# Loading one of four weight blocks through ScalarE's DMA queue in place of SyncE's, at the start of a gated attention and gMLP kernel

## The chip, the cores and the metric

The kernel runs on one core of one Trainium2 chip. The metric is the device time of one execution in microseconds. A profiled execution also has a span, from its first to its last instruction; where both are known, the time is the span plus about 1.7 us (206.23 against 204.5 in the profiled execution of before).

Every trace here shows a mean granted TensorE clock of 0.998 or more. All timed runs count as fast.

## The reference, cut to what matters

```python
g = sigmoid((x * gate_w).sum(-1, keepdims=True))
a = A(x)                       # linear attention with softmax features, 32 heads
z = gelu(x @ w_in)             # [2048, 512] @ [512, 1376]
z1, z2 = z[..., :688], layernorm(z[..., 688:])
b = (z1 * (w_sp @ z2 + b_sp)) @ w_out
out = g * a + (1 - g) * b
```

The experiment concerns only the first step: the columns 688 to 1375 of `w_in`, which give `z2`. They are loaded in four blocks of 128 rows, and a tile is 128 rows of x.

## The kernel before

Five kinds of data are needed at the start: tiles 0 and 1 of x (loaded as they are and transposed on TensorE), four blocks of w_in, the gate row, tiles 2 and 3 of x (transposed by the DMA itself), and the other half of w_in. Two engines issue these transfers, SyncE (`nc.sync`) and ScalarE (`nc.scalar`).

```python
def load_z2w(eng, dt):                                     # L117
    eng.dma_start(out=w_z2[:, dt, 0:FH], in_=w_in_v[:, dt, FH:F])

nc.sync.dma_start(out=xs[:, 0, :], in_=x2[0:P, :])         # L119
nc.scalar.dma_start(out=xs[:, 1, :], in_=x2[P:2 * P, :])   # L120
load_z2w(nc.sync, 0)
load_z2w(nc.scalar, 1)
load_z2w(nc.sync, 2)
nc.scalar.dma_start(out=gaterow[0:NDT, :], in_=gate_w...)  # L124
load_z2w(nc.sync, 3)
nc.scalar.activation(out=scrap[:, :], ..., func=AF.Gelu_apprx_tanh)   # L127, loads the table
x_dma_T(2, 2)                                              # L131, x tiles 2 and 3
for h in range(2):
    nc.sync.dma_start(out=w_z1[:, 2*h:2*h+2, :], ...)      # L135, the other half of w_in
...
```

TensorE first runs seven dummy matmuls (L222), then transposes x tiles 0 and 1 (L280). It then works through the blocks in their order, for both tiles, and goes on to tile 2 (matmuls of L191 and L230):

```python
warm_up(6); warm_up(1, P)
x_T(0, ...); x_T(1, ...)
one(0, 0, 0); z_part(0, 0, HF, True); gate_T()     # one(tile, block, half)
one(0, 1, 0); one(1, 0, 0); z_part(1, 0, HF, True); one(1, 1, 0)
... one(tt, 1, 1) ...                              # block 1
... one(tt, 2, 0); one(tt, 2, 1); z_part ...       # block 2
... one(tt, 3, 0); one(tt, 3, 1); z2_out ...       # block 3
z2_tile(2); z2_tile(3)                             # needs the DMA transpose of L131
```

The softmax here doesn't subtract the row's maximum and nothing guards it: scores larger than these inputs give would overflow.

Of the kernel before, what the change touches and what calls it, by code (L numbers as in the profile page):

```python
# [35 lines left out]
def kernel(  # L36
# [14 lines left out]
    nc = tc.nc  # L51
# [64 lines left out]
    def load_z2w(eng, dt):  # L116
        eng.dma_start(out=w_z2[:, dt, 0:FH], in_=w_in_v[:, dt, FH:F])  # L117
# [4 lines left out]
    load_z2w(nc.scalar, 1)  # L122
    load_z2w(nc.sync, 2)
    nc.scalar.dma_start(out=gaterow[0:NDT, :], in_=gate_w.rearrange("(dt p) -> dt p", p=P))  # L124
    load_z2w(nc.sync, 3)
    scrap = early.tile([P, 1], BF16, name="scrap")
    nc.scalar.activation(  # L127
        out=scrap[:, :], in_=nc.const_aps.tensor(1.0, [P, 1], BF16), func=AF.Gelu_apprx_tanh)
# [515 lines left out]
```

## Time and profile before

| | before |
|---|---|
| median of the three runs known before the prediction | 206.92 us (206.57 to 206.94) |
| span of the profiled execution | 204.5 us |
| TensorE busy | 200.6 us, 98% |
| transpose of x tiles 2 and 3 issued / landed | 2.67 / 7.23 us |
| tile 2 starts on TensorE | 7.27 us |

Times inside an execution count from its first instruction. A landing is the moment at which a transfer's semaphore is complete. Landings are given to 0.01 us from the records of the trace; the DMA view rounds the time from issue to landing to 0.1 us. The profiled execution of before took 206.23 us.

### The profile page before, as it was taken

What the parts mean: (1) busy time and instruction counts of PE and PEld (TensorE: products, weight loads), DVE (VectorE), ACT (ScalarE), POOL (GpSimd) and SP (SyncE); (2) the same over time, 40 slices, a digit from 0 to 9 for tenths busy, and PEclk for the clock granted to TensorE, in tenths of its full rate; (3) what the DMA queues carried; (4) which work ended last, traced back from release to release, by engine and by line L of the source; (5) the groups of instructions that cost most, each with busy time, mean ns of one, the idle gap of its engine ahead of it and who ended that gap; (6) DMA issues with size and microseconds to landing.
All of it is one profiled execution on the core that took longest, in us unless ns stands there. A gap on an engine that the chain in (4) does not pass through costs nothing.

```text
span 204.5 us, 3996 instructions
## 1 busy us (share of the span) xinstructions
PE 200.6 (98%) x1557; PEld 119.5 (58%) x1557; DVE 130.5 (64%) x283; ACT 74.6 (36%) x122; POOL 45.8 (22%) x76
## 2 busy tenths in 40 slices
PE   8999999999999999999999999999999999999994
PEld 3566666655665555656565666555555555665642
DVE  4567484837977587979797788555566645633332
ACT  3466678796222333332424042222251136002303
POOL 3020202021523325334242442222204220200000
PEclk9999999999999999999999999999999999999999
DMA  5998599999997017950422229763567458552943
GB/s 188 247 209 151 117 277 209 241 194 234 207 290 168 3 38 148 317 97 15 77 47 46 51 38 114 142 126 62 108 161 79 90 112 184 61 96 51 141 80 104
DMA packets 89931, 27.22 MB, mean 133 GB/s; under 512 B 84184, under 2 KB 89912, under 8 KB 89912
## 3 DMA queue, kind: packets, MB, share of 16 engines
q1 hardware_dynamic: 87744, 24.99, 64.1%
q10 hardware_dynamic: 2168, 1.98, 3.6%
q8 instruction: 12, 0.20, 0.4%
q14 instruction: 7, 0.06, 0.1%
HBM read 4.15 MB, written 2.10 MB: 31 GB/s over the span
## 4 chain that ended last, share of the span: by engine, by line
PE 95%; DMA 2%; SPq 1%; DVE 0%; issue 0%
PE mm L454 37%; PE zp L191 17%; PE mm L355 14%; PE mm L515 8%; PE mm L509 7%; PE mm L395 7%; DMA xT<-in_A_x_dram 2%; PE kvacc L411 2%; PE at L467 2%; PE mm L520 1%; SPq L117 1%; PE zp L307 0%; PE at L478 0%; SPq L119 0%; PE pq L307 0%; DVE ob L527 0%
## 5 line engine op out<-in xcount | busy, mean ns | idle before, releaser
L454 PE MATMUL mm<-z2all,wspT 128*128 128x344 bf16 x512 | 79.9, 309 | 0.0
L454 PEld LDWEIGHTS <-wspT 128*128 128x128 bf16 x512 | 49.0, 98 | 25.3
L191 PE MATMUL zp<-w_z,xT 128*128 128x344 bf16 (+1 forms) x254 | 38.2, 309 | 0.3 <-DMA xT<-in_A_x_dram 0.3
L359 ACT ACTIVATE eq<-mm 128x512 bf16<-128x512 f32 x32 | 17.4, 594 | 51.4 <-PE mm L355 25.7
L363 DVE TENSOR_REDUCE zs<-eq 128x64 f32<-128x1024 bf16 x16 | 19.5, 1220 | 20.1 <-ACT eq L359 20.1
L191 PEld LDWEIGHTS <-xT 128*128 128x128 bf16 x254 | 24.3, 98 | 12.4 <-DMA xT<-in_A_x_dram 0.6
L359 ACT ACTIVATE ek<-mm 128x512 bf16<-128x512 f32 x32 | 17.3, 600 | 27.1 <-PE mm L355 27.1
L459 DVE SCALAR_TENSOR_TENSOR ucat<-mm,bT,z1all 128x344 bf16<-128x344 f32 x32 | 17.4, 544 | 15.1 <-PE mm L454 15.1
L372 POOL TENSOR_TENSOR eq<-eq,ratio 128x512 bf16<-128x512 bf16 x16 | 16.9, 1059 | 44.6 <-DVE ratio L371 36.6
L531 ACT ACTIVATE ob<-mm,g_inv 128x512 bf16<-128x512 f32 (+1 forms) x15 | 10.1, 680 | 33.1 <-PE mm L520 28.5
L363 DVE TENSOR_REDUCE zs<-ek 128x64 f32<-128x1024 bf16 x16 | 19.3, 1209 | 2.8 <-ACT ek L359 2.8
L515 PE MATMUL mm<-wspT,uT 128*128 128x512 bf16 (+2 forms) x85 | 20.1, 367 | 0.0
L355 PEld LDWEIGHTS <-xT 128*128 128x128 bf16 x128 | 12.2, 98 | 12.0
L372 POOL TENSOR_TENSOR ek<-ek,ratio 128x512 bf16<-128x512 bf16 x16 | 16.9, 1059 | 2.2 <-DVE ratio L371 1.7
L509 PE MATMUL mm<-wspT,oT 128*128 128x512 bf16 (+2 forms) x68 | 16.6, 366 | 0.0
L355 PE MATMUL mm<-wq_p,xT 128*128 128x512 bf16 x64 | 16.4, 379 | 0.0
L395 PE MATMUL mm<-wv_sb,xT 128*128 128x512 bf16 x64 | 16.4, 379 | 0.0
L355 PE MATMUL mm<-wk_p,xT 128*128 128x512 bf16 x64 | 16.3, 379 | 0.0
L209 DVE BATCH_NORM_STATS2 bn<-z2all 128x6 f32<-128x344 bf16 x32 | 14.9, 501 | 0.0
L206 ACT ACTIVATE z2all<-zp 128x688 bf16<-128x688 f32 x16 | 11.8, 744 | 7.6 <-PE zp L191 7.6
L260 ACT ACTIVATE z1all<-zp 128x688 bf16<-128x688 f32 x16 | 11.9, 744 | 5.1 <-PE zp L191 4.6
L515 PEld LDWEIGHTS <-uT 128*128 128x128 bf16 x85 | 8.1, 98 | 9.4 <-issue 0.2
(77 smaller groups left out, 141.8 us busy)
## 6 DMA issues: line engine op xcount, KB each, us to landing
out_dram<-ob ACTq DMA_DIRECT2D x12, 128.0 KB, 2.7
wspT<-in_B_w_out_dram SPq DMA_DIRECT2D x2, 640.0 KB, 5.5
w_z<-in_B_w_in_dram SPq DMA_DIRECT2D x2, 344.0 KB, 4.8
w_z<-in_B_w_in_dram SPq DMA_DIRECT2D x3, 172.0 KB, 3.6
wv_sb<-in_A_wqkv_dram SPq DMA_DIRECT2D x2, 256.0 KB, 4.0
wspT<-in_A_wo_dram SPq DMA_DIRECT2D x2, 256.0 KB, 4.1
out_dram<-ob SPq DMA_DIRECT2D x3, 128.0 KB, 1.8
uT<-ucat SPq DMA_TRANSPOSE x16, 2.8
```

Source lines behind the costliest of these rows:

```text
L191: nc.tensor.matmul(zp[:, j, 0:n], lhsT=xT[:, dt, tt * P:(tt + 1) * P], rhs=wt[:, dt, j * HF:j * HF + n], start=(dt == 0), stop=(dt == NDT ...
L209: nc.vector.bn_stats(out=bn6[:, tt, j, :], in_=z2v[:, j, :])
L260: nc.scalar.activation(out=z1all[:, tt, :].rearrange("p (j n) -> p j n", j=2), in_=zp[:, :, 0:HF], func=AF.Gelu_apprx_tanh,)
L355: nc.tensor.matmul(ps[:, :], lhsT=xT[:, dt, tt * P:(tt + 1) * P], rhs=w[:, dt, :], start=(dt == 0), stop=(dt == NDT - 1))
L359: nc.scalar.activation(out=e[:, :, a, :], in_=ps[:, :].rearrange("p (h f) -> p h f", f=DH), func=AF.Exp, scale=1.0 - 2.0 * a)
L363: nc.vector.tensor_reduce(out=z[:].rearrange("p h a -> p (h a)"), in_=e[:].rearrange("p h a f -> p (h a) f"), axis=AX.X, op=ALU.add,)
L372: nc.gpsimd.tensor_tensor(out=e[:, :, 1, :], in0=e[:, :, 1, :], in1=ratio[:, :, None].to_broadcast([P, H, DH]), op=ALU.mult)
L395: nc.tensor.matmul(v_ps[:, :], lhsT=xT[:, dt, tt * P:(tt + 1) * P], rhs=wv_sb[:, dt, :], start=(dt == 0), stop=(dt == NDT - 1))
L454: nc.tensor.matmul(gp[:, 0:HF], lhsT=wspT[:, st, tt * P:(tt + 1) * P], rhs=z2all[:, st, j * HF:(j + 1) * HF], start=(st == 0), stop=(st == ...
L459: nc.vector.scalar_tensor_tensor(out=ucat[tt % NU][:, c0 + j * HF:c0 + (j + 1) * HF], in0=gp[:, 0:HF], scalar=bT[:, tt:tt + 1], in1=z1all[ ...
L509: nc.tensor.matmul(acc, lhsT=oTs[tt][:, g, :], rhs=wo_t[:, g, c0:c1], start=start and g == 0, stop=stop and g == NG - 1)
L515: nc.tensor.matmul(acc, lhsT=uTs[tt][:, i + ft, :], rhs=w_main[i][:, ft, c0:c1], start=start and ft == 0, stop=False)
```

## The change

The change wants to take one issue of 0.43 us off SyncE, so that the transpose for x tiles 2 and 3 and everything behind it is issued earlier.

```diff
     nc.scalar.dma_start(out=gaterow[0:NDT, :], in_=gate_w.rearrange("(dt p) -> dt p", p=P))
-    load_z2w(nc.sync, 3)
+    load_z2w(nc.scalar, 3)
```

## The prediction

> **What bounds the kernel now.** I read the page first: its engine shares, its slices and its chain of work.
>
> ```profile
> span 204.5 us, 3996 instructions
> PE 200.6 (98%) x1557; PEld 119.5 (58%) x1557; DVE 130.5 (64%) x283; ACT 74.6 (36%) x122; POOL 45.8 (22%) x76
> ...
> PE 95%; DMA 2%; SPq 1%; DVE 0%; issue 0%
> ```
>
> TensorE is busy for 200.6 us of 204.5, and the chain that ended last lies on it for 95%. Only 2% of the chain is a DMA and 1% SyncE's issuing, and both are in the first microseconds. So the second view is the chain of waits in the window from 0 to 8 us (start, duration, what).
>
> ```profile
> 0.81 0.40 SPq L119
> 1.21 0.06 issue
> 1.26 0.42 SPq L117
> 1.68 0.05 issue
> 1.73 0.42 SPq L117
> 2.15 0.04 issue
> 2.20 0.43 SPq L117
> 2.63 0.04 issue
> 2.67 4.55 DMA xT<-in_A_x_dram
> 7.23 0.05 issue
> 7.27 0.76 PE zp L191 x4
> ```
>
> SyncE issues one load of x and then blocks 0, 2 and 3 of w_in, at 1.26, 1.73 and 2.20 us. Only then, at 2.67, does it issue the transpose that loads x tiles 2 and 3. That transpose lands at 7.23, and TensorE starts tile 2 at 7.27. The issue of block 3, 0.43 us and a gap of 0.04, is thus a link of the chain, and it is what the change takes out.
>
> How much is there to gain? The third view is the timeline of TensorE around that point.
>
> ```profile
> 5.17 0.89 PE L191 MATMUL zp<-w_z,xT 128*128 128x344 bf16 x5
> ...
> 6.25 0.74 PE L191 MATMUL zp<-w_z,xT 128*128 128x344 bf16 x4
> 7.27 0.91 PE L191 MATMUL zp<-w_z,xT 128*128 128x344 bf16 x5 [0.28 <-DMA xT<-in_A_x_dram]
> ```
>
> The page shows 309 ns for one such matmul, but they overlap: four take 0.74 us, so one starts every (0.74 - 0.31) / 3 = 0.144 us. The last of the four started at 6.25 + 3 x 0.144 = 6.68 and its successor could have started at 6.83. It started at 7.27. The stall is therefore 7.27 - 6.83 = 0.44 us, not just the 0.28 us of visible idle. The table of waits of TensorE has only one other entry, 0.8 us before the first instruction. The windows view has TensorE busy for 16.53 us of the 16.53 us from 7.27 to 23.80, and for 60.00 of the 60.00 us from 40 to 100. What is won at 7.27 has no later wait to vanish in. Its most is 0.44 us, 0.2% of the time.
>
> [...] The trace has this time: 0.42 us for a load of 172 KB. So I count no bandwidth as won. [...] The DMA view from 2 to 4 us agrees with the sharing:
>
> ```profile
> q1 hardware_dynamic: 284, 0.31, 50.7%
> q10 hardware_dynamic: 281, 0.30, 41.8%
> ```
>
> q1 is SyncE's queue and q10 ScalarE's: with work in both they moved 0.31 and 0.30 MB. [...] the trace has 1.28 us for it at 2.35 us. I need that number because the change pushes this load back.
>
> **The change part by part.** The order view (before against after) shows 3116 rows on TensorE, all alike, and no difference on VectorE and GpSimd. On SyncE three loads in a row become two; on ScalarE one load appears between the gate row and the table load. Bytes, tiles and matmuls are the same. The waits that the later SyncE issues carry are the same too.
>
> Removed from SyncE: one issue, 0.43 + 0.04 = 0.47 us. The transpose is then issued at 2.67 - 0.47 = 2.20. Its issue lasts 1.45 us, to 3.65. The next issue, half of the other weights, waits for both loads of x; these land 2.7 and 2.9 us after 0.81 and 0.80, so at 3.5 and 3.7. It moves from 4.17 to about 3.70. If the landing moves with the issue, tile 2 is there at 7.23 - 0.47 = 6.76, just ahead of the 6.83 at which TensorE could use it, and the whole 0.44 us is won.
>
> Added to ScalarE:
>
> ```profile
> 1.24 0.47 ACTq L117 DMA_DIRECT2D w_z<-in_B_w_in_dram  x1
> 1.75 0.57 ACTq L124 DMA_DIRECT2D gaterow<-in_gate_w_dram  x1
> 2.35 1.28 ACT L127 ACT_TABLE_LOAD   x1 [2.35 <-DVE ident L112]
> 3.65 0.21 ACT L127 ACTIVATE scrap<-const-bfloat16-1.0 128x1 bf16<-128x1 bf16 x1
> 4.46 0.37 ACT L283 COPY xT<-pq 128x256 bf16<-128x256 bf16 x1 [0.61 <-PE pq L280]
> ```
>
> The issue of block 3 stands at about 2.35 and takes 0.47 us by the row of block 1. The table load goes to 2.35 + 0.50 = 2.85, ends at 4.13, and the scrap activation ends at about 4.36. ScalarE's first useful work, the copy of x, starts at 4.46 after an idle 0.61 us. The 0.50 us fits into that idle time with 0.1 us to spare. ScalarE costs nothing.
>
> Moved: block 3 is issued at 2.35 in place of 2.20, 0.15 us later, on the other queue. This is the delicate part. It landed 4.0 us after its issue, at 6.2, and TensorE's first matmul on it is the first of the four at 6.25: there is almost no slack. But those 4.0 us are largely queueing: block 3 stood behind blocks 0 and 2 on SyncE's queue. Block 1 on ScalarE's queue landed 3.3 us after its issue at 1.24, so at 4.5, and from 4.0 to 4.5 us that queue had only 6.1% of the DMA engines, against 98.9% for SyncE's. Block 3 behind it finds its own queue nearly empty and gets half the engines. With 3.3 to 3.6 us it lands at 5.65 to 5.95, in time for 6.25.
>
> The one that pays is block 2, which now shares. It landed 3.6 us after 1.73, at 5.3; its first matmul is the fourth of the five from 5.17, at 5.17 + 3 x 0.145 = 5.60. Half of the engines for its remaining packets costs it at most its own transfer time alone, an estimate of 172 KB (176,000 bytes) at the 319 GB/s that the DMA view has from 4.0 to 4.5 us: 0.55 us. From 0.0 to 0.5 us later is 5.3 to 5.8, so the stall there is 0 to 0.2 us. It delays the end of the first two tiles from 6.83 to at most 7.03.
>
> The sum: TensorE can go on at 6.83 to 7.03, tile 2 lands at 6.8 to 7.0 (it too shares with block 3, and its packets are many and small). The later of the two is about 6.95 to 7.0, against 7.27: 0.3 us won, of a possible 0.44.
>
> **The rivals.** First, a wait that takes the place: block 3 lands late on ScalarE's queue, or block 2 is pushed behind it. For it speak the two thin margins, 0.05 us for block 3 and 0.3 us for block 2; against it the empty queue. If block 3 needs its old 4.0 us from 2.35 it lands at 6.35 and costs 0.1 us; if ScalarE's queue is 0.5 us worse, the gain of the transpose is cancelled: 206.9 to 207.1 us. Second, a landing that does not move: the transpose is held by the DMA engines and not by its issue. From 4.5 to 5.5 us they are near full, and the same bytes stand ahead of it. But from 5.5 to 6.0 us the DMA view has only 0.04 MB moved, 89 GB/s, in the middle of this transpose, [...] this speaks for the issue. If it does not move the time stays at 206.9. Third, a full gain of 0.44 us: 206.5 us.
>
> **How range and chances follow.** The median before is 206.92 us, but its three runs spread from 206.57 to 206.94, so its middle is nearer 206.8 and the spread is as large as the effect. 206.92 - 0.3 = 206.62; I say 206.65. The best case is 206.57 - 0.44 = 206.13 and the bad one 206.94 + 0.2 = 207.1; neither end is likely, and the range is 206.25 to 207.05. 2% is 4.1 us, nine times the largest gain that I found and far more than a late block could cost, so I give 98% to within 2% and 1% to each side.
>
> **What would show the steps right or wrong.** Right: the transpose is issued at about 2.20 and lands at 6.7 to 7.0; TensorE's wait on x before tile 2 shrinks from 0.28 us to under 0.1 or is gone; block 3 lands before 6.0; the ScalarE copy of x still starts at 4.4 to 4.5. Wrong: a TensorE wait on w_z appears near 5.6 (block 2) or 6.3 (block 3); the transpose still lands at 7.2; or the copy of x starts after 4.6 behind the table load. A change of over 0.5 us in either direction would mean that the chain after 7.27 changed as well, which I see no reason for.

The 0.42 us for a load of 172 KB is the time of one issue on SyncE. That no bandwidth is won was an assumption at that point. The 1.28 us at 2.35 us is the table load of L127 (ACT_TABLE_LOAD). That the dip to 89 GB/s speaks for the issue was not shown. Two more steps are my estimates: that a queue with work beside the other gets half of the engines, from the 50.7% and 41.8% above, and that block 3's 4.0 us are largely queueing, from block 1's 3.3 us on the other queue. "Near full" from 4.5 to 5.5 us is 267 GB/s in the DMA view, and that the transpose's packets are small shows from 5.5 to 6 us: 142 of 148 packets are under 512 bytes.

## The result, and the profile after

| | median, us | executions | range |
|---|---|---|---|
| before | 206.66 | 6 | 206.34 to 206.94 |
| changed | 206.19 | 6 | 205.97 to 206.46 |

The ratio is 0.9978, with a 95% interval of 0.9965 to 0.9991. Ratios are the mean time of one kernel's fast runs over that of the other's of the same rounds, so they are not quite the ratio of the medians quoted beside them. By the means, 206.20 against 206.66, the gain is 0.46 us. The six runs of before include the three that were known.

The trace tells another story. The page of the changed kernel has the same span and the same chain share:

```profile
span 204.5 us, 3978 instructions
...
PE 199.6 (98%) x1539; PEld 119.7 (59%) x1557; DVE 130.4 (64%) x283; ACT 74.6 (36%) x122; POOL 45.7 (22%) x76
...
PE 95%; DMA 2%; issue 1%; SPq 0%; DVE 0%
```

The 18 instructions and 1.0 us of TensorE that are missing are matmul records lost from the trace: weight loads are 1557 in both. The chain of waits of the changed kernel from 0 to 9 us (start, duration, what):

```profile
1.26 0.41 SPq L117
1.67 0.05 issue
1.72 4.29 DMA w_z<-in_B_w_in_dram
6.01 0.04 issue
6.05 0.45 PE zp L191 x2
```

The link that waited for the transpose has gone. In its place stands the load issued at 1.72 us, block 2, which now takes 4.29 us to land. The timelines of SyncE, ScalarE and TensorE show the rest:

```profile
2.18 1.43 SPq L131 DMA_TRANSPOSE xT<-in_A_x_dram  x1
...
2.34 0.37 ACTq L117 DMA_DIRECT2D w_z<-in_B_w_in_dram  x1
2.74 1.28 ACT L127 ACT_TABLE_LOAD   x1 [2.74 <-DVE ident L112]
...
4.40 0.37 ACT L283 COPY xT<-pq 128x256 bf16<-128x256 bf16 x1 [0.16 <-PE pq L280]
...
5.36 1.14 PE L191 MATMUL zp<-w_z,xT 128*128 128x344 bf16 x5
6.69 2.50 PE L191 MATMUL zp<-w_z,xT 128*128 128x344 bf16 x16
```

The transpose is issued at 2.18 in place of 2.67. ScalarE's copy of x starts at 4.40, so ScalarE pays nothing. The five matmuls from 5.36, which took 0.89 us before, take 1.14: the fourth of them waits for block 2. Sixteen matmuls run from 6.69 without a break, four on block 3 and then tile 2, which therefore starts at 6.69 + 4 x 0.145 = 7.27. That is the very time of before. The transpose had landed at 7.14, just before it was needed. (The first weight load of tile 2, which the table below lists, is at 7.18 here, 0.09 us ahead of that matmul.)

So one pair of traces shows no gain at all in the first 8 us and equal spans. The times show one of 0.46 us. Either the profiled execution of before was a lucky one, or the six runs of one kernel were.

### The profile page after: what moved, and what is told of

It reads as the page before. It is cut to its first block, busy times and chain, and to the rows that moved or that the text cites. A ratio compares the mean times of both kernels' runs of the same rounds, so it can differ in the third digit from the quotient of the medians.

```text
span 204.5 us, 3978 instructions
## 1 busy us (share of the span) xinstructions
PE 199.6 (98%) x1539; PEld 119.7 (59%) x1557; DVE 130.4 (64%) x283; ACT 74.6 (36%) x122; POOL 45.7 (22%) x76
## 4 chain that ended last, share of the span: by engine, by line
PE 95%; DMA 2%; issue 1%; SPq 0%; DVE 0%
PE mm L454 37%; PE zp L191 18%; PE mm L355 13%; PE mm L515 8%; PE mm L395 7%; PE mm L509 7%; DMA w_z<-in_B_w_in_dram 2%; PE kvacc L411 2%; PE at L467 2%; PE mm L520 1%; PE zp L307 0%; PE at L478 0%; SPq L117 0%; SPq L119 0%; PE pq L307 0%
## 5 line engine op out<-in xcount | busy, mean ns | idle before, releaser
L191 PE MATMUL zp<-w_z,xT 128*128 128x344 bf16 (+1 forms) x254 | 38.1, 310 | 0.3 <-DMA w_z<-in_B_w_in_dram 0.3
L509 PE MATMUL mm<-wspT,oT 128*128 128x512 bf16 (+2 forms) x61 | 15.6, 365 | 0.4
```

Of the source, the lines that this page charges most:

```text
L191: nc.tensor.matmul(zp[:, j, 0:n], lhsT=xT[:, dt, tt * P:(tt + 1) * P], rhs=wt[:, dt, j * HF:j * HF + n], start=(dt == 0), stop=(dt == NDT ...
L509: nc.tensor.matmul(acc, lhsT=oTs[tt][:, g, :], rhs=wo_t[:, g, c0:c1], start=start and g == 0, stop=stop and g == NG - 1)
```

## The experiments

My theories at the start were these. Theory A: the gain is real and comes from the earlier issue on SyncE. Theory B: it is real and comes from the second queue. Theory C: there is no such gain; the first stage varies from one execution to the next, and the comparison caught that.

Eighteen traces came of it. The table has the landings of the first stage, the pace of TensorE's first real matmuls (full, or half as explained below), the first weight load of tile 2, and the span. "T" is the transpose of x tiles 2 and 3. In the three rows of the exchange, block 3 goes by SyncE and block 2 by ScalarE.

| trace | T issued | block 0 | block 2 | block 3 | T landed | pace | tile 2 | span |
|---|---|---|---|---|---|---|---|---|
| before | 2.67 | 4.38 | 5.36 | 6.17 | 7.23 | full | 7.27 | 204.5 |
| b_again (before) | 2.67 | 4.50 | 5.23 | 5.66 | 6.70 | full | 6.81 | 204.2 |
| b_third (before) | 2.66 | 4.40 | 5.37 | 5.95 | 7.04 | full | 7.08 | 204.4 |
| after | 2.18 | 4.57 | 6.01 | 6.29 | 7.14 | full | 7.18 | 204.5 |
| a_again (changed) | 2.19 | 4.52 | 5.81 | 6.01 | 6.97 | half | 7.47 | 204.9 |
| a_third (changed) | 2.20 | 4.54 | 6.05 | 6.28 | 7.21 | full | 7.25 | 204.6 |
| a_fourth (changed) | 2.20 | 4.48 | 6.10 | 6.26 | 7.17 | half | 7.63 | 205.0 |
| a_wait | 2.39 | 4.58 | 5.65 | 5.84 | 6.88 | full | 7.00 | 204.4 |
| b_wait | 2.85 | 4.89 | 5.41 | 5.89 | 6.94 | full | 7.20 | 204.6 |
| b_wait2 | 3.28 | 4.48 | 5.25 | 5.85 | 7.14 | half | 7.46 | 204.8 |
| late3 | 2.18 | 4.73 | 5.36 | 7.09 | 6.34 | half | 7.83 | 205.2 |
| late3_b | 2.19 | 4.58 | 5.18 | 8.25 | 6.19 | full | 8.73 | 206.1 |
| swap23 | 2.19 | 4.28 | 5.79 | 5.12 | 6.70 | half | 7.45 | 204.8 |
| swap23_b | 2.19 | 4.21 | 5.84 | 5.66 | 6.80 | full | 6.96 | 204.4 |
| swap23_c | 2.18 | 4.48 | 6.52 | 6.00 | 7.55 | full | 7.63 | 205.0 |
| b_busy | 2.66 | 4.16 | 5.65 | 6.10 | 7.20 | full | 7.24 | 204.5 |
| a_busy | 2.20 | 4.35 | 5.88 | 6.13 | 7.03 | full | 7.19 | 204.6 |
| b_cold | 2.67 | 4.42 | 5.62 | 6.11 | 7.13 | half | 8.76 | 206.2 |

The last two columns differ by 197.2 to 197.4 us in every row. After tile 2 the executions agree within 0.2 us and nothing is given back: the differences between them are made in the first 9 us.

### Both kernels again, unchanged

`b_again` and `b_third` are the kernel before, `a_again`, `a_third` and `a_fourth` the changed one; there is no edit.

> The kernel before, unchanged, against itself: what the comparison gives where nothing is changed, and a second profile. If the forecast failed because the first profile of before was a lucky execution (206.23 us, while the six timed ones are 206.34 to 206.94), this profile shows a longer stall at the start: tile 2 starts at 7.5 to 7.8 in place of 7.27. Ratio expected 1.000 within 0.001. If the first profile was typical, tile 2 starts again at 7.2 to 7.3 and the gain of 0.46 us lies elsewhere than in the first 8 us.

> The changed kernel again, unchanged. All theories: ratio 0.998 within 0.001 if the gain is real; if it was a chance of the six runs, 1.000. In the profile: the two-queue theory and the issue theory both have tile 2 start at 6.9 to 7.3, with the transpose for x tiles 2 and 3 issued at 2.2.

> The changed kernel, unchanged, once more with many runs of before on the same chip. From the six traces so far I hold that the first stage ends at the latest of four things: block 0 landing + 2.31 us, block 2 landing + 1.17, block 3 landing + 0.5, the transpose landing + 0.04, plus up to 0.5 us when TensorE's clock is still at half rate after 4.5 us; and that these move by up to 0.5 us from one execution to the next in both kernels. Then the means of many runs differ by 0 to 0.2 us: ratio 0.999 to 1.000. If the 0.46 us of the first comparison was the change's own, ratio 0.998 again.

> The same as the run before it, for a second profile and more runs in the mean: ratio 0.999 to 1.000 and block 2 landing at 5.6 to 6.0 us (5.2 to 5.4 in the three traces with the old order), the transpose at 6.9 to 7.2 although it is issued at 2.2.

> A third look at the kernel before. The model of the first stage expects tile 2 at the latest of block 0 + 2.31, block 2 + 1.17, block 3 + 0.5 and transpose + 0.04 us if the transposes on TensorE stand in pairs of 0.27 us, and 0.4 to 0.7 us later than block 0 + 2.31 if they stand in pairs of 0.42 us (half rate). The span should be tile 2's start plus 197.6 to 197.8 us.

| run | mean, us | before in the same rounds, mean | ratio | 95% interval |
|---|---|---|---|---|
| b_again | 206.53 | 206.48 (11 runs) | 1.0001 | 0.9979 to 1.0023 |
| a_again | 206.51 | 206.48 (11 runs) | 0.9999 | 0.9977 to 1.0022 |
| a_third | 206.61 | 206.48 (11 runs) | 1.0005 | 0.9990 to 1.0020 |
| a_fourth | 206.35 | 206.48 (11 runs) | 0.9992 | 0.9974 to 1.0010 |

The gain did not come back. In these rounds the 18 executions of the changed kernel have a mean of 206.49 us, and the 28 of before 206.49 as well. One execution scatters by 0.31 us (changed) and 0.34 us (before) as a standard deviation, so the difference of the two means is known to sqrt(0.31^2/18 + 0.34^2/28) = 0.10 us, and a gain of 0.46 is excluded here. With the first comparison added it is 206.42 (24 runs) against 206.52 (34 runs): 0.10 us with 0.17 on either side. Theory C holds, and a gain of up to some 0.27 us can be neither shown nor excluded. (Eleven more runs of before, in the last rounds, are left out here, since the changed kernel did not run beside them: their mean is 206.70, or 206.46 without one of 209.02.)

My own guess on how it failed was also wrong. I expected a second trace of before to show a later tile 2 than 7.27, since the profiled execution had been faster than its timed runs. It showed 6.81. What ends its first stage is not the transpose but block 0, by the chain of waits of `b_again`:

```profile
1.26 3.24 DMA w_z<-in_B_w_in_dram
4.50 0.04 issue
4.55 0.31 PE zp L191
```

Block 0 landed at 4.50, and TensorE then ran to tile 2 without a stall, because the transpose landed at 6.70. With one and the same program the transpose landed at 7.23, 6.70 and 7.04 in three traces. That scatter is larger than the whole gain that I had forecast.

From the traces up to then I made a model of the first stage at full pace: tile 2's weight load starts at the latest of block 0 + 2.31, block 2 + 1.17, block 3 + 0.5 and T + 0.04 us. The offsets are the matmuls between the landing and tile 2. `b_third` tests it on a trace that it was not made from: 6.71, 6.54, 6.45 and 7.08 give 7.08, and 7.08 it is. That tests the transpose's term alone. Where block 2 comes last, the model is some 0.05 us high (7.01 for 6.96 in `swap23_b`, 7.69 for 7.63 in `swap23_c`), and it knows nothing of the gate row: in `a_wait` a TensorE instruction waited for that load, and tile 2 came at 7.00 where the model gives 6.92. It is good to about 0.1 us. (My expectation there of the rest of the span, 197.6 to 197.8, was a slip; it is 197.3 as in the others.)

### TensorE's pace in the first stage

The traces of `a_again` and `a_fourth` don't obey the model: tile 2 is later than any landing explains. The same pair of matmuls, on block 1 and block 0, in the timeline of TensorE of before:

```profile
4.73 0.45 PE L191 MATMUL zp<-w_z,xT 128*128 128x344 bf16 x2
```

and of `a_again`:

```profile
5.16 0.73 PE L191 MATMUL zp<-w_z,xT 128*128 128x344 bf16 x2
```

The first of the pair takes 0.31 us in before and 0.44 in `a_again`. In `a_fourth`, where the slow stretch is longer, such matmuls start at 5.35, 5.64, 5.93 and 6.21, 0.29 us apart, against 0.145 us in before: TensorE runs at half its rate, in `a_again` until about 5.9 us. So the traces show two rates, and the moment of the switch differs between executions of one program: `a_third` and `after`, the same kernel, had the full rate from their first real matmul on. Of the 15 traces with the usual warm-up, five were at half pace when the first real matmuls came: two of the changed kernel's four, none of the three of before, and three of experiments.

The packed traces hold the clock's own records, which no view prints as they are. The first record, a switch to full clock, stands at 3.53 to 4.49 us in the full-pace traces that have one (3.76 in before), at 6.05, 6.29 and 6.44 in `swap23`, `a_fourth` and `late3`, and at 8.72 in `b_cold` below. The full clock then lasts 201.386 us in the first group and 197.973 in the others; in before it outlasts the span of 204.5 us, 3.76 + 201.386 = 205.15. The mean granted clock leaves out what lies before the first record: it is 1.000 in before, although the first record is at 3.76. `a_again`, `b_wait2` and `late3_b` have no clock record, and it says 1.000 for `a_again` as well, and 1.00 from 4 to 6 us alone. The 0.998 of `swap23`, `a_fourth` and `late3` comes from a drop to half at 204.02 to 204.41 us, just before their end.

That makes a mean below 1.000 a marker of late switches, though not of all of them, in the timed runs without a trace. In the rounds above, 8 of the 28 executions of before have it, with a mean of 206.89 us against 206.33 for the other 20, and 3 of the 18 of the changed kernel, 206.77 against 206.44. So late switches come in both kernels and are a part of their scatter.

> The kernel before with two warm-up matmuls in place of seven, so that TensorE idles from about 1.3 to 3.5 us. If the half rate at the start is a matter of how busy TensorE was just before, every execution has it now, and longer: the transposes in pairs of 0.42 us, matmuls of 344 columns every 0.28 us until 6.5 us or later, tile 2 at 7.8 to 8.6, and the time 0.7 to 1.5 us above before: ratio 1.003 to 1.007. If the rate has nothing to do with it, ratio 1.000.

```diff
-        warm_up(6)
+        warm_up(1)
```

`b_cold` has two dummy matmuls in place of seven, and TensorE idles until 3.56 us. From its timeline:

```profile
5.87 1.65 PE L191 MATMUL zp<-w_z,xT 128*128 128x344 bf16 x5
```

Five such matmuls took 0.89 us in before. The half pace lasts to about 8.5 us, tile 2 starts at 8.76, and the ratio is 1.0042 (1.0000 to 1.0084). That is what the first of the two expectations said, with tile 2 a little later than its 7.8 to 8.6; the interval is wide because one run of before in these rounds took 209.02 us. The transpose landed at 7.13 here, and nobody waited for it.

> The kernel before with six more dummy matmuls on TensorE: one of 512 columns at the end of the warm-up and five of 128 columns between the transposes of x and the first real matmul, where it idles for 0.3 to 0.5 us twice. In four of ten traces TensorE ran its first two tiles at half rate until 5.9 to 6.4 us (transposes in pairs of 0.42 us in place of 0.27), and the time of one execution varies by 1 us. If those idle gaps are what keeps the half rate on, the profile shows the pairs at 0.27 and the mean falls by 0.1 to 0.2 us with a smaller spread: ratio 0.999 to 0.9995. If the switch depends on when the execution starts and not on the gaps, ratio 1.000 to 1.001 with the same spread.

> The changed kernel with the same six dummy matmuls. If the clock is what hides the change, here the landings set the end of the first stage and the two busy kernels differ by what the landings differ: block 2 lands 0.6 us later and the transpose as before, so a_busy is equal to or up to 0.2 us slower than b_busy. If the change has a gain of its own of 0.46 us that the slow clock hides at times, a_busy is 0.3 to 0.5 us faster than b_busy.

```diff
-        warm_up(6)
+        warm_up(7)
...
-        one(0, 0, 0)
+        warm_up(5, P); one(0, 0, 0)
```

With the two idle gaps filled, both traces switched to full pace by 4.3 us (the clock's records say 3.95 and 4.14). The times did not profit: `b_busy` 206.50 us on the mean, ratio 0.9993 (0.9950 to 1.0037), `a_busy` 206.74, 1.0003 (0.9962 to 1.0043). The filling itself moved the first real matmul to 4.86 and 4.92 us, and the spread did not shrink (206.23 to 207.29, and 206.09 to 207.32). Whether the gaps decide the switch stays open after two traces. The changed kernel is again not the faster one.

### Does the landing of the transpose follow its issue?

> The changed kernel, but the transpose for x tiles 2 and 3 may not be issued before GpSimd has zeroed its target, at about 2.55 to 2.6 us, 0.4 us later than in the changed kernel and about where the kernel before issues it. Block 3 still goes by ScalarE. Theory A (the gain is the earlier issue of the transpose and of what follows it on SyncE): most of the gain goes, ratio 0.9995 to 1.0. Theory B (the gain is block 3 on the second queue, which no longer stands between block 2 and the transpose): the gain stays, ratio 0.998.

```diff
-    x_dma_T(2, 2)
+    nc.gpsimd.memset(xT[:, :, 2 * P:4 * P], 0.0); x_dma_T(2, 2)
```

> The kernel before, with two such zeroings on GpSimd ahead of the transpose, so that it is issued at about 3.05 to 3.2, 0.4 to 0.5 us later than in before. Theory A: the time rises by the same 0.4 to 0.5 us, ratio 1.002 or more. Theory B (the queue or another landing sets the end of the first stage): it rises by less than 0.2 us, ratio below 1.001.

```diff
-    x_dma_T(2, 2)
+    nc.gpsimd.memset(xT[:, 0:2, 4 * P:6 * P], 0.0); nc.gpsimd.memset(xT[:, :, 2 * P:4 * P], 0.0); x_dma_T(2, 2)
```

> The kernel before with a longer hold: the transpose is issued at 3.3 to 3.4 us, 0.7 us later than in before (the hold of the earlier run moved it by only 0.18). If the landing follows the issue it lands at 7.4 to 7.9 and the time rises by 0.3 to 0.7 us, ratio 1.0015 to 1.0035. If the DMA engines set the landing, with slack in the issue, it lands at or before 7.3 and the ratio stays below 1.001.

```diff
+    nc.gpsimd.memset(xT[:, :, 4 * P:6 * P], 0.0); nc.gpsimd.memset(xT[:, :, 2 * P:4 * P], 0.0)
+    with tc.manual_schedule(engines={mybir.EngineType.SP}):     # keeps the order of the loads that follow
         x_dma_T(2, 2)
         ...
```

The zeroing on GpSimd writes what the transpose will overwrite, so the transpose must wait for it. GpSimd was quicker than I had reckoned, and the first two holds came out short: 2.39 us in `a_wait` (I expected 2.6) and 2.85 in `b_wait` (3.05 to 3.2). The third is long enough, by the timeline of SyncE of `b_wait2`:

```profile
3.28 1.33 SPq L131 DMA_TRANSPOSE xT<-in_A_x_dram  x1
```

| run | T issued | T landed | mean, us | ratio to before | 95% interval |
|---|---|---|---|---|---|
| a_wait | 2.39 | 6.88 | 206.53 | 1.0001 | 0.9978 to 1.0025 |
| b_wait | 2.85 | 6.94 | 206.14 | 0.9982 | 0.9961 to 1.0004 |
| b_wait2 | 3.28 | 7.14 | 206.27 | 0.9988 | 0.9972 to 1.0004 |

Theory A falls. Issued 0.6 us later than in before, the transpose lands within the range that before shows by itself, and the time does not rise. Both held kernels even have means below before, with 1 inside both intervals; I claim no gain from that. Over all rows of the table with the same bytes ahead of the transpose and the usual queues (before, changed and the three holds), its issue ranges over 1.1 us, from 2.18 to 3.28, and its landing over 6.70 to 7.23, without one following the other: four changed traces average 7.12, three of before 6.99. Nor do its packets come earlier. They are under 512 bytes (from 5.5 to 6 us in before, 142 of the 148 packets), like some tens of small ones of other transfers. Of that size the DMA view counts, from 4 to 5 us, 82 in before, 73 in the changed kernel and 60 in `b_wait2`, with the issue at 2.67, 2.18 and 3.28.

### What sets the landing of the transpose

> Block 3 goes by SyncE again, but after the transpose, which is then issued at 2.2 us as in the changed kernel, with 172 KB less ahead of it in the DMA queues. If the bytes ahead of the transpose set its landing, and not its issue, it lands 0.4 to 0.6 us earlier than in the changed kernel, at 6.3 to 6.6. If the transpose's landing cannot move, it lands at 6.9 to 7.2 again. Block 3, behind it, is late: landing at 6.8 to 7.2, so the first stage ends at 7.3 to 7.7 and the time is 0.2 to 0.6 us above before, ratio 1.001 to 1.003.

> A second look at block 3 behind the transpose on SyncE. If the bytes ahead of the transpose set its landing, it lands at 6.2 to 6.7 us again (6.34 before), and block 2, which shares with nothing on ScalarE's queue, at 5.2 to 5.6. If the 6.34 was chance, the transpose lands at 6.9 to 7.2.

```diff
-    load_z2w(nc.sync, 3)
...
     x_dma_T(2, 2)
+    load_z2w(nc.sync, 3)
```

In `late3` the transpose is issued at 2.18, as in the changed kernel, but block 3's 172 KB are behind it, neither ahead of it nor beside it on ScalarE's queue. It landed at 6.34 and 6.19 us, against 6.97 to 7.21 in the four traces of the changed kernel: 0.86 us earlier on the mean at the same issue. From 4 to 5 us, 480 and 560 packets under 512 bytes moved, against the 60 to 82 above. So the bytes ahead of the transpose or beside it hold it. The DMA view from 4 to 5.5 us shows engines that are busy with them (the share adds up the time of the packets, so at 122.8% some packets of one engine overlap). Before:

```profile
DMA packets 656, 0.43 MB, mean 285 GB/s; under 512 B 416, under 2 KB 656, under 8 KB 656
...
q1 hardware_dynamic: 641, 0.42, 122.8%
q10 hardware_dynamic: 15, 0.01, 2.0%
```

Changed:

```profile
DMA packets 599, 0.43 MB, mean 284 GB/s; under 512 B 347, under 2 KB 599, under 8 KB 599
...
q1 hardware_dynamic: 442, 0.24, 78.0%
q10 hardware_dynamic: 157, 0.19, 38.1%
```

The DMA engines move the same 0.43 MB in both. The change only hands 0.18 MB of them from SyncE's queue (q1) to ScalarE's (q10). So the prediction was right to count no bandwidth as won: 285 GB/s before, 284 changed.

The bytes don't explain the scatter from one execution to the next, and there the dip that the prediction saw comes in. From 5.5 to 6 us, in the midst of the transpose, the DMA view has 286 GB/s in `b_again`, 189 in `b_third` and 89 in before, and the transpose landed at 6.70, 7.04 and 7.23. The changed kernel has the dip too, 127 to 187 GB/s in its four traces, although its issue of the transpose was over by 3.6 us. So the dip does not go with the issue; its cause stays open.

`late3` itself does not win, since block 3 is now late. Its ratio is 1.0015 (0.9996 to 1.0033), and in `late3_b` TensorE stands still for it, by its timeline:

```profile
8.29 0.89 PE L191 MATMUL zp<-w_z,xT 128*128 128x344 bf16 x5 [1.70 <-DMA w_z<-in_B_w_in_dram]
```

Block 3 landed at 8.25 there, and the model's block 3 + 0.5 gives 8.75 for tile 2; it started at 8.73. In `late3` the half pace hid the same wait: block 3 landed at 7.09, and TensorE had no use for it before 7.39.

### What delays block 2

> The changed kernel with blocks 2 and 3 exchanged: block 3 by SyncE at 1.7 us, block 2 by ScalarE behind the gate row at 2.3. If what delays the load on SyncE is that ScalarE's queue shares the DMA engines with it, block 3 lands at 5.7 to 6.1 as block 2 did in the changed kernel, and block 2 at 6.0 to 6.3; TensorE needs block 2 first, so tile 2 starts at block 2 plus 1.17, at 7.2 to 7.5 or later: 0.1 to 0.4 us slower than before, ratio 1.0005 to 1.002. If block 2 lands at 5.4 here, the delay belongs to block 2 and not to the sharing.

> A second look at the exchange of blocks 2 and 3. In six traces with block 3 on ScalarE, SyncE's second block landed at 5.65 to 6.10 us; in the one of the exchange it landed at 5.12. If sharing with ScalarE's queue is what delays it, 5.12 was a lucky execution and this one has 5.6 to 6.1. If the delay belongs to block 2's own data, SyncE's second block (block 3 here) lands at 5.0 to 5.4 again.

> A third look at the same, with the same two expectations: 5.6 to 6.1 us if sharing delays the load, 5.0 to 5.4 if it is block 2's own data.

```diff
-    load_z2w(nc.sync, 2)
     nc.scalar.dma_start(out=gaterow[0:NDT, :], ...)
+    load_z2w(nc.scalar, 2)
     load_z2w(nc.sync, 3)
```

Block 2 is SyncE's second weight load, issued at 1.72 us in both kernels. It landed at 5.23 to 5.37 in the three traces of before and at 5.81 to 6.10 in the four of the changed kernel. Either sharing with block 3 on ScalarE's queue delays it, or it is block 2's own data. The exchange puts block 3 in its place. That load landed at 5.12, 5.66 and 6.00 us. The first fits block 2's own data, the other two fit the sharing. And in `late3` and `late3_b`, where ScalarE's queue has no third large load, block 2 landed at 5.36 and 5.18. Sharing is the reading that fits eleven of these twelve traces (three of before, four changed, two of `late3`, three exchanged); the 5.12 is unexplained. The other traces of the table blur it. With the order of before, block 2 landed at 5.41 and 5.25 in `b_wait` and `b_wait2`, but at 5.65 and 5.62 in `b_busy` and `b_cold`; with block 3 on ScalarE's queue at 5.65 in `a_wait` and 5.88 in `a_busy`. Over all nine traces without the sharing and six with it the means are 5.38 and 5.92, and the two groups touch at 5.65. So sharing costs block 2 some 0.5 us on the mean, and one execution can be as late without it.

The cost of a late block is plain in `swap23_c`, where block 2 landed at 6.52 us:

```profile
6.56 0.45 PE L191 MATMUL zp<-w_z,xT 128*128 128x344 bf16 x2 [0.69 <-DMA w_z<-in_B_w_in_dram]
```

Over six timed executions the exchange had 206.60 us, ratio 0.9996 (0.9958 to 1.0034): no better and no worse. No kernel that I tried beats before beyond its scatter, so there is no better version to report.

## Why the prediction was right or wrong

- **What bounds the kernel, and that nothing later takes a gain back:** right. Span less tile 2's start is 197.2 to 197.4 us in all 18 traces.
- **The issue moves from 2.67 to 2.20, and the next one from 4.17 to 3.70:** right, 2.18 and 3.67.
- **ScalarE costs nothing:** right. The copy of x stood at 4.40 us, behind a table load of 1.28 us as reckoned.
- **"If the landing moves with the issue, tile 2 is there at 7.23 - 0.47 = 6.76":** this step failed. The landing does not follow the issue. It lay at 6.97 to 7.21 in four changed traces, and a hold of 0.6 us did not move it either. Fewer bytes ahead of it or beside it moved it by 0.86 us. My second rival said so, and the argument that I set against it, the dip to 89 GB/s, did not carry: the dip stayed when the issue came earlier.
- **"Block 3 lands at 5.65 to 5.95":** wrong, 6.01 to 6.29 in the four traces. It needed 3.7 to 4.0 us on ScalarE's queue, not 3.3 to 3.6. I gave it half the engines; from 4 to 5.5 us its queue had 38.1% of them against 78.0% for SyncE's.
- **"0.0 to 0.5 us later", the stall on block 2:** that block 2 pays was right, and the term was mis-sized. Block 2 landed at 5.81 to 6.10, 0.67 us later on the mean (5.99 against 5.32). In the first trace after, the fourth of the five matmuls started at 6.05 and not at 5.36 + 3 x 0.145 = 5.80: 0.25 us. So in that trace my first rival came true beside the second, with the sign that I had named for it, a wait on w_z for block 2.
- **The sum, 0.3 us:** not there. Over 24 and 34 executions it is 0.10 us, with 0.17 on either side.
- **The number and the range:** the first comparison gave 206.19 us, 0.06 below the range's low end. Two things failed in that step. I took 206.92, the median of three runs, for the kernel's time, where later runs give 206.5 on the mean. And the low end rested on "neither end is likely", where single executions of both kernels range from 205.7 to 207.0 us (and one lay at 209.02). The later means of the changed kernel, 206.35 to 206.61, lie inside the range, but not for the reason that I gave.
- **Within 2%:** right.

What stays open is why six executions of each kernel differed by 0.46 us the first time. The standard error of such a difference is sqrt(0.31^2/6 + 0.33^2/6) = 0.18 us, so chance makes it rarely, though not never. The share of half-pace executions in each six could do it: none of the changed kernel's six has a mean clock below 1.000. But the clock of the six of before is not on record, and only one of the twelve left a trace, so that is argued and not shown. Nor does the record say on which chip the first comparison ran; the later ones ran on four.

## What to carry to other kernels

Here an issue 0.47 us earlier brought no earlier landing: 7.12 us on the mean of four traces, against 6.99 of three. Before counting on an earlier issue, hold it back on purpose or take away the bytes ahead of it: the hold of 0.6 us did not delay this landing, and 172 KB less ahead of it or beside it brought it 0.86 us earlier. The second issuing queue only changed whose bytes waited, with 0.43 MB moved either way from 4 to 5.5 us. And several transfers arrived here within some tenths of a microsecond of their use: block 0, block 2 or the transpose came last from one execution to the next (`b_again`, `after`, before). So a gain below the scatter of one execution, 0.34 us in before, needs the kernel before measured against itself first.
